# A new written order of the arithmetic: 39 crossbar entries in place of 24, and eleven stores on ScalarE's queue

## The chip, the core and the metric

The kernel runs on one core of a Trainium2 chip. The metric is the device time of one execution in microseconds; lower is better. The time before is the median of three runs.

The engines are named as the profile names them: PE is TensorE (PEld its weight loads), DVE is VectorE, ACT is ScalarE, POOL is GpSimd, SP is SyncE, which here does nothing but issue transfers. A name with a q (SPq, ACTq) is the part of an engine that issues transfers.

## The reference

Two layers follow each other. The first is a recurrence over 768 tokens, for 4 batches and 8 heads of width 40:

```python
for t in range(S):
    y[:, :, t] = np.einsum('bhd,bhde->bhe', rt, state)
    Sa = np.einsum('bhde,bhe->bhd', state, at)
    state_decay = state * wt[:, :, None, :] - np.einsum('bhd,bhe->bhde', Sa, bt)
    state = state_decay + np.einsum('bhd,bhe->bhde', vt, kt)
```

The second takes x, the heads side by side (4 x 768 x 320), and mixes tokens and channels:

```python
theta = x @ w_theta
zr, zi = x * np.cos(theta), x * np.sin(theta)
y = np.einsum('ts,bsd->btd', w_tok_r, zr) + np.einsum('ts,bsd->btd', w_tok_i, zi)
u = x + y
out = u + np.maximum(u @ w_ch, 0.0)
```

## The kernel before

Tokens are cut into chunks of 128, six for each batch, 24 in all, numbered 0 to 23. For each chunk the recurrence becomes matrix products: the inputs are scaled by running products of w (sums of logarithms, taken by matmul, then exponentials), transposed, multiplied to 128 x 128 score matrices (psi, phi, lamv, lamu), masked to a triangle, and used to form x0, nu, the new state gt and the output y. The state gt links a chunk to the next of its batch. The second layer follows for each chunk: theta, sine and cosine, z; when all six chunks of a batch have their z, the token mixing YR sums over them; then u, the channel product CH and the output.

What sets the order is one string, `ORDER`. An entry is a step, a chunk, an engine and a PSUM bank: `EVT:23S` is the step EVT of chunk 23 on SP; A is ACT, V is DVE, G is POOL, @n is a bank. The program walks the string once and emits each step's instructions; every engine then executes its own in that order and waits only for data and for free buffers. So the string sets what stands in front of what on each engine, and nothing else does.

A transpose can be made in two ways. On TensorE it is two entries: for v, `TRV` emits four 128 x 128 transposes into PSUM and `EVT` with A or V copies them out. With S there is no TRV; `EVT` is one crossbar transfer on SP (`dma_start_transpose`), from SBUF to SBUF. The same choice exists for nu (`NUT`, `ENUT`, four transposes), x (`XT`, `EXT`, three), u (`UT`, `EUT`, two for an even chunk and three for an odd one, which share the middle block), k and b (`TRK`, `EKBT`, eight), and the state (`GD`, `EGD`, four small matmuls). In the profile TensorE's transposes are those of line 316 (all other matmuls have line 312), and crossbar transfers stand at L488, L536 (v) and L701 (x and u).

`ST` stores a chunk's output `oo`, line 780, always on SP. Loads are `LDK`, `LDB`, `LDV`, `LDW`, `LDR` on SP and `LDA` mostly on ACT (lines 343 to 368). The order of all transfers is kept as written; an engine that comes to a transfer whose data are not ready waits there, with everything that stands behind it.

The helper that puts a transfer on an engine, and the choice of engine:

```python
def queue(e):
    return nc.scalar if e == "A" else nc.sync
```

Of the kernel before, what the change touches and what calls it, by code (L numbers as in the profile page):

```python
# [20 lines left out]
LDW:2 LN:2A LDW:0 CSI:2@1 LDK:0 INVW:2A CSE:2@0 LDA:1 LDC:0.0G LDC:0.2G CST:2 LN:0A WI:2A CSE:0@1  # L21
CST:0 LDA:0 CSI:0@0 WI:0A LDB:0 AH:1V LDB:1 LDK:1 LDK:2 AH:0V INVW:0A TRA:1@0 EAT:1V LDB:2 LDV:0
TRA:0@0 EAT:0A KH:0V TRK:0@3 KH:1V TRK:1@0 LDR:0 KH:2G LDA:2 EKBT:1A EKBT:0V PSI:0@0 PHI:0@1 EPSI:0V
LDV:1 LDB:3 CV:0A EPHI:0A LDK:3 LDA:3A MPHI:0G TRV:0@3 AH:2G X0:0@2 CR:0G LDV:2 ENX:0V PSI:1@0
PHI:1@1 LDW:4 NU:0 EVT:0V EPSI:1A ENU:0V LDR:2 TRK:2@0 EPHI:1V CV:1A EKBT:2A TRA:2@2 MPSI:1G EAT:2A
TRR:0@1 NUT:0@0 LDA:4A GT:0@2 ENUT:0V LDB:4 PSI:2@0 ERT:0A PHI:2@1 EGT:0V X0:1@0 LDK:4 GD:0@3 KH:3G
EPSI:2A EPHI:2V ENX:1A LDV:3 TRV:1@2 LDB:5 ERT:1A EGD:0A LV:0@0 CV:2A EVT:1V NU:1 ENU:1V LU:0@1
GT:1@1 GI:1 AH:3G ELU:0A LN:4A NUT:1@3 MPSI:2G TRV:2@2 LDA:5A MLU:0G LDK:5 TRA:3@0 ELV:0V ENUT:1V
LV:1@0 EAT:3V LU:1@1 LDR:4 EGT:1V TRK:3@3 GD:1@1 LDW:6 X0:2@0 ELV:1A ELU:1V EGD:1A EKBT:3V CR:2G
CSI:4@0 MLV:1G Y:0@1 ENX:2A INVW:4A NU:2 KH:4G EX:0V CSE:4@1 PSI:3@0 ENU:2A EVT:2A CST:4 WI:4A  # L30
TRR:2@1 LDA:6A GT:2@2 EPSI:3V NUT:2@3 ERT:2A ENUT:2V PHI:3@1 GI:2 ERT:3A AH:4G XT:0@3 CV:3G LU:2@0
EPHI:3V TRK:4@1 LV:2@1 AH:5G LDV:4 TRA:4@0 EXT:0A EGT:2V ELU:2A X0:3@2 TRV:3@3 LDK:6 EKBT:4A ELV:2V
ENX:3A LDB:6 Y:1@1 EAT:4A NU:3 PHI:4@0 ENU:3A EVT:3A MLU:2G PSI:4@1 EX:1V CR:4G NUT:3@2 EPHI:4V
KH:5G EPSI:4A LDV:5 LDK:7 ENUT:3A GT:3@1 MPSI:4G XT:1@0 Y:2@3 EGA:3V LV:3@0 EX:2V EGT:3V LU:3@1
EXT:1A TRR:4@0 TRA:5@1 ELV:3A LN:6A GD:3@2 TRK:5@3 ELU:3V EKBT:5A CSI:6@1 LDB:7 CV:4G ERT:4V EAT:5A
CSE:6@0 INVW:6A X0:4@3 GD:2@1 LDR:6 ENX:4A CST:6 ERT:5V WI:6A EGD:3V TRV:4@0 MLV:3G LDA:7A EGD:2V
EVT:4V KH:6G NU:4 AH:6G ENU:4A CV:5A PHI:5@1 PSI:5@0 EPSI:5A LDW:8 GT:4@2 EPHI:5V NUT:4@1 ENUT:4V
# [18 lines left out]
TRV:10@2 CR:10A EGT:9V TH:7@0 EPHI:10V EPSI:10V YR:0.4 ZR:5G ETH:7A TRR:10@1 LDK:12 EVT:10A LU:9@1
TRA:11@0 KH:11G CW:2.0G ERT:10A Y:8@2 EAT:11V YR:0.5 X0:10@0 LDB:12 ERT:11V LDV:11 LV:10@0 ELU:9A
EU:0V ENX:10A TRK:11@1 LN:12A NU:10 ELV:10V TH:6@3 CSE:12@1 CW:2.1G MLU:9G EX:8V ENU:10A EKBT:11V
CSI:12@0 CST:12 LDW:14 LDK:13 ETH:6A GT:10@2 WT:2.1@3 INVW:12A LDB:13 WI:12A WT:2.0@1 EWT:2.1V
EGA:10V LDA:13A Y:9@0 EWT:2.0A NUT:10@3 XT:8@1 PHI:11@1 KH:12G EGT:10V EXT:8A LDT:3.0 ENUT:10A  # L60
# [75 lines left out]
def kernel(  # L136
# [198 lines left out]
    def queue(e):  # L335
        return nc.scalar if e == "A" else nc.sync
# [569 lines left out]
```

## Time and profile before

| | us |
|---|---|
| median of 3 runs (202.24 to 202.73) | 202.59 |
| the profiled execution | 202.4 |
| its span | 200.7 |
| TensorE busy, share of the span | 186.6, 93% |
| VectorE busy | 168.7, 84% |
| ScalarE busy | 149.2, 74% |
| GpSimd busy | 146.5, 73% |

The busy time of TensorE contains overlap: matmuls are pipelined, so the pitch between two of them, and not the duration of one, says how much of the engine's queue each takes. A row of the timeline is: start, duration, engine, line, operation, written tile <- read tiles, shapes, count, and in brackets the idle time of the engine just before and what ended it. For an SPq or ACTq row the duration is that of issuing, not of the transfer. A row of a table of stretches is: from and to, length, then for each engine busy time and number of instructions, then granted TensorE clock, DMA share and GB/s. A row of waits is: who waited, for whom, microseconds in total, times, the longest. The granted clock was 1.00 throughout.

### The profile page before, as it was taken

To read this page: it belongs to the slowest core of one execution; us is meant where nothing else is said; L and a number is where in the kernel's file an instruction comes from. 1 tells how busy PE (TensorE), PEld (TensorE's weight loads), DVE (VectorE), ACT (ScalarE), POOL (GpSimd) and SP (SyncE) were. 2 spreads that over 40 slices of the span, in tenths; PEclk is the share of its full clock that TensorE was granted. 3 is DMA by queue.
4 is the path that set the end of the run, shared out by engine and by line. 5 is a ranking of instruction groups with operands and counts; after the bars stand their busy time and mean duration, and the time that the engine had idled before them with its cause. 6 is when DMAs were issued, how large, how long until landed. Compare 5 with 4: busy or idle time off the path is not lost.

```text
span 200.7 us, 7824 instructions
## 1 busy us (share of the span) xinstructions
PE 186.6 (93%) x3278; PEld 147.8 (74%) x3278; DVE 168.7 (84%) x319; ACT 149.2 (74%) x278; POOL 146.5 (73%) x155
## 2 busy tenths in 40 slices
PE   0769999999999999999999999999999999999992
PEld 0357788787888888888787878887877878776670
DVE  7257899899999998999899899899999876862682
ACT  4626999999999888898989686978688922682310
POOL 8118699789799998978998996963975986466000
PEclk9999999999999999999999999999999999999999
DMA  6999999999999999999987999994783596433434
GB/s 156 178 201 193 205 170 222 162 237 171 209 210 242 207 249 197 245 233 226 252 201 124 224 210 175 187 199 94 157 191 86 128 186 138 106 79 92 144 121 158
DMA packets 141955, 35.95 MB, mean 179 GB/s; under 512 B 136352, under 2 KB 140384, under 8 KB 141920
## 3 DMA queue, kind: packets, MB, share of 16 engines
q1 hardware_dynamic: 120064, 31.57, 76.8%
q10 hardware_dynamic: 20800, 3.28, 10.9%
q0 software_dynamic: 1056, 0.61, 2.3%
q8 instruction: 25, 0.41, 0.9%
q14 instruction: 10, 0.08, 0.1%
HBM read 29.54 MB, written 3.93 MB: 167 GB/s over the span
## 4 chain that ended last, share of the span: by engine, by line
PE 83%; SPq 5%; DVE 5%; DMA 4%; issue 1%; ACT 0%; DVEq 0%; ACTq 0%
PE sm L312 42%; PE sm L316 21%; PE sc L312 20%; DMA raw_kb<-in_k_dram 3%; SPq L363 1%; SPq L780 1%; DVE psi L309 1%; DMA xT<-x_two 1%; DVE phi L309 1%; SPq L368 1%; SPq L701 1%; DVE lamv L309 1%; DVE lamu L309 1%; SPq L357 1%; DVE kb L309 0%
## 5 line engine op out<-in xcount | busy, mean ns | idle before, releaser
L309 POOL TENSOR_TENSOR kb<-raw_kb,invW_two 128x640 bf16<-128x640 f32 x22 | 33.9, 1541 | 15.8 <-DMA raw_kb<-in_b_dram 8.2
L312 PE MATMUL sm<-z,wtok_r 128*128 128x320 bf16 x120 | 34.5, 300 | 0.0
L312 PE MATMUL sm<-z,wtok_i 128*128 128x320 bf16 x120 | 34.4, 299 | 0.0
L309 POOL TENSOR_TENSOR z<-cs,x_two 128x640 bf16<-128x640 f32 x22 | 30.8, 1402 | 2.2 <-ACT cs L739 1.9
L309 POOL TENSOR_TENSOR ah<-raw_a,Wi_two 128x320 bf16<-128x320 f32 x22 | 19.0, 864 | 8.5 <-issue 4.2
L309 DVE TENSOR_TENSOR psi<-sc,mask_p 128x1024 bf16<-128x1024 f32 x18 | 21.9, 1217 | 1.5 <-PE sc L312 1.5
L309 DVE TENSOR_TENSOR phi<-sc,mask_p 128x1024 bf16<-128x1024 f32 x16 | 19.5, 1219 | 1.6 <-PE sc L312 1.3
L309 DVE TENSOR_TENSOR lamu<-sc,mask_p 128x1024 bf16<-128x1024 f32 x15 | 18.3, 1219 | 0.5 <-PE sc L312 0.3
L312 PE MATMUL sc<-aT,kbT 64*128 64x128 bf16 x384 | 17.5, 225 | 0.0
L312 PEld LDWEIGHTS <-wtok_r 128*128 128x128 bf16 x144 | 14.0, 98 | 4.6
L312 PEld LDWEIGHTS <-wtok_i 128*128 128x128 bf16 x144 | 14.1, 98 | 3.4
L299 ACT COPY rvT<-sm 128x512 bf16<-128x512 bf16 (+1 forms) x26 | 12.7, 500 | 5.0 <-PE sm L316 4.9
L316 PE MATMUL sm<-ident,kb 128*128 128x128 bf16 x184 | 15.3, 231 | 1.1 <-DVE kb L309 1.1
L312 PE MATMUL sm<-kb,lamv 128*128 128x40 bf16 x192 | 15.0, 180 | 0.0
L312 PE MATMUL sm<-kb,lamu 128*128 128x40 bf16 x192 | 14.9, 179 | 0.0
L309 DVE TENSOR_TENSOR lamv<-sc,mask_p 128x1024 bf16<-128x1024 f32 x12 | 14.6, 1219 | 0.3
L312 PEld LDWEIGHTS <-rvT 64*128 64x128 bf16 (+1 forms) x272 | 13.5, 95 | 1.8 <-issue 0.3
L312 PEld LDWEIGHTS <-kbT 64*128 64x128 bf16 x384 | 11.8, 98 | 4.0 <-issue 2.3
L312 PE MATMUL sm<-wth,xT 128*128 128x320 bf16 x72 | 13.6, 300 | 0.8 <-DMA xT<-x_two 0.8
L776 DVE SCALAR_TENSOR_TENSOR oo<-sm,u_two 128x320 f32<-128x320 f32 x24 | 10.9, 489 | 3.6 <-PE sm L312 3.5
L309 DVE TENSOR_TENSOR x_two<-sm,Wi_two 128x320 bf16<-128x320 f32 x24 | 11.7, 486 | 2.5 <-PE sm L312 2.4
L594 POOL TENSOR_SCALAR_AFFINE_SELECT lamv<-lamv 128x1024 bf16<-128x1024 bf16 x12 | 13.1, 1092 | 0.9 <-ACT lamv L299 0.7
(137 smaller groups left out, 607.2 us busy)
## 6 DMA issues: line engine op xcount, KB each, us to landing
raw_w_two<-in_w_dram SPq DMA_DIRECT2D x12, 320.0 KB, 5.1
raw_kb<-in_k_dram SPq DMA_DIRECT2D x24, 160.0 KB, 5.0
raw_kb<-in_b_dram SPq DMA_DIRECT2D x24, 160.0 KB, 4.5
raw_v<-in_v_dram SPq DMA_DIRECT2D x24, 160.0 KB, 5.1
raw_r_two<-in_r_dram SPq DMA_DIRECT2D x12, 320.0 KB, 4.8
out_dram<-oo SPq DMA_DIRECT2D x24, 160.0 KB, 2.1
raw_a<-in_a_dram ACTq DMA_DIRECT2D x20, 160.0 KB, 4.7
wtok_raw<-in_moe_w_tok_r_dram SPq DMA_DIRECT2D x6, 384.0 KB, 4.9
```

Source lines behind the costliest of these rows:

```text
L299: keep(nc.scalar.copy(out=out, in_=in_))
L309: keep(eng[e].tensor_tensor(out=out, in0=in0, in1=in1, op=ALU.mult))
L312: keep(nc.tensor.matmul(out, lhsT=lhsT, rhs=rhs, start=start, stop=stop, skip_group_check=True))
L316: keep(nc.tensor.transpose(out=out, in_=in_, identity=ident))
L357: transfer(queue(e).dma_start(out=t, in_=two_of(w, i)))
L363: transfer(queue(e).dma_start(out=tiles[i].raw_kb[:, j], in_=source(ap, i)))
L368: transfer(queue(e).dma_start(out=t, in_=source(ap, i)))
L594: keep(nc.gpsimd.affine_select(out=flat, in_=flat, compare_op=ALU.is_ge, fill=0.0, base=-1, pattern=[[0, 2 * G], [1, 128]], channel_multip ...
L701: transfer(nc.sync.dma_start_transpose(out=t[:, 0:n], in_=held))
L776: keep(nc.vector.scalar_tensor_tensor(out=q.oo, in0=q.ops[:, 0:DM], scalar=0.0, in1=q.u, op0=ALU.max, op1=ALU.add))
L780: transfer(nc.sync.dma_start(out=out_r[i // NCH, i % NCH], in_=tiles[i].oo))
```

## The change

The string `ORDER` is replaced, so the arithmetic of all engines is written in another order, and `store` takes an engine. The order of the loads and the queues they are on are kept. Counted over the string:

- Crossbar entries (S): 39 in place of 24. v: chunks 18 to 23 (before 23 alone). nu: 18, 20, 21, 22 (before 20, 22). u: 2 and 4 to 18 (before 2, 10, 13 to 17 and 20). x: 13, 15 to 19, 21, 23 (before 15, 17 to 23). The states of 18, 20, 21, 22 and kb of 21 as before.
- TensorE has 48 transposes less: its queue has 6462 rows in place of 6558, a weight load and a matmul for each.
- Stores: eleven of 24 (chunks 1, 3, 4, 6, 7, 10, 12, 15, 16, 19, 23) on ACT, the rest on SP.
- Some evictions and products change their engine; two products ah go from DVE to POOL. The number of activation-table loads on ACT is 14 in both.

```diff
-LDW:2 LN:2A LDW:0 CSI:2@1 LDK:0 INVW:2A CSE:2@0 LDA:1 LDC:0.0G LDC:0.2G CST:2 LN:0A WI:2A CSE:0@1
...
+LDW:2 LN:2A LDW:0 CSE:2@1 LDK:0 LN:0A CST:2 CSE:0@0 CST:0 WI:2A CSI:2@1 LDA:1 LDC:0.0G LDC:0.2G
...
-    def store(i):
-        transfer(nc.sync.dma_start(out=out_r[i // NCH, i % NCH], in_=tiles[i].oo))
+    def store(i, e):
+        transfer(queue(e).dma_start(out=out_r[i // NCH, i % NCH], in_=tiles[i].oo))
...
-        "ST": lambda i, j, e, b: store(i),
+        "ST": lambda i, j, e, b: store(i, e),
```

Three places show what moves. First, VectorE at the beginning, from its first product on (kb_97 and ah_95 belong to chunk 0, kb_98 and ah_96 to chunk 1). Before:

```order
L309 TENSOR_TENSOR ah_96<-raw_a,Wi_two 128x8x40
L309 TENSOR_TENSOR ah_95<-raw_a,Wi_two 128x8x40
L301 COPY aT<-sm_276 128x512
L309 TENSOR_TENSOR kb_97<-raw_kb,invW_two 128x16x40
L309 TENSOR_TENSOR kb_98<-raw_kb,invW_two 128x16x40
L301 COPY kbT<-sm_294 128x1024
L309 TENSOR_TENSOR psi<-sc_322,mask_p 128x1024
```

Now:

```order
L308 TENSOR_TENSOR kb_97<-raw_kb,invW_two 128x16x40
L308 TENSOR_TENSOR kb_98<-raw_kb,invW_two 128x16x40
L308 TENSOR_TENSOR psi<-sc_311,mask_p 128x1024
L308 TENSOR_TENSOR phi<-sc_327,mask_p 128x1024
L308 TENSOR_TENSOR phi<-sc_382,mask_p 128x1024
```

The products ah have gone to GpSimd, and the copies of chunk 0's aT and kbT to ScalarE; between the two kb and the first psi VectorE has no copy any more.

Second, SyncE's queue in the stretch with the loads of chunks 20 and 21 (raw_kb_3765 in the old program and raw_kb_3757 in the new one are chunk 20's k and b, raw_kb_3839 and raw_kb_3943 chunk 21's). Before:

```order
L363 DMA raw_kb_3765<-in_k_dram 128x8x40
L368 DMA raw_v_3811<-in_v_dram 128x8x40
L701 DMA_TRANSPOSE xT_3826<-x_two_1_112 128x3x128
L363 DMA raw_kb_3765<-in_b_dram 128x8x40
L363 DMA raw_kb_3839<-in_b_dram 128x8x40
L780 DMA out_0_dram<-oo_3319 128x320
L363 DMA raw_kb_3839<-in_k_dram 128x8x40
L343 DMA raw_r_two_3980<-in_r_dram 128x8x80
```

Now:

```order
L362 DMA raw_kb_3757<-in_k_dram 128x8x40
L367 DMA raw_v_3771<-in_v_dram 128x8x40
L700 DMA_TRANSPOSE xT_3796<-x_two_1_112 128x3x128
L362 DMA raw_kb_3757<-in_b_dram 128x8x40
L700 DMA_TRANSPOSE uT_3854<-u_two_0_117 128x3x128
L700 DMA_TRANSPOSE uT_3861<-u_two_0_117 128x2x128
L487 DMA_TRANSPOSE nuT_3864<-nu_0_107 128x4x128
L535 DMA_TRANSPOSE rvT_3887<-v_3_106 128x4x128
L362 DMA raw_kb_3943<-in_b_dram 128x8x40
L362 DMA raw_kb_3943<-in_k_dram 128x8x40
L700 DMA_TRANSPOSE xT_3984<-x_two_2_113 128x3x128
L342 DMA raw_r_two_3986<-in_r_dram 128x8x80
```

Four more crossbar transfers now stand between chunk 20's b and chunk 21's, a fifth behind them, and the store between chunk 21's b and k is gone.

Third, SyncE's queue near the end, from chunk 14's and 15's u on (x_two_5_116 holds the x of chunks 22 and 23). Before:

```order
L701 DMA_TRANSPOSE uT_4952<-u_two_1_118 128x2x128
L701 DMA_TRANSPOSE uT_4957<-u_two_1_118 128x3x128
L701 DMA_TRANSPOSE xT_4999<-x_two_5_116 128x3x128
L780 DMA out_0_dram<-oo_4941 128x320
L780 DMA out_0_dram<-oo_4423 128x320
L701 DMA_TRANSPOSE xT_5077<-x_two_5_116 128x3x128
```

Now:

```order
L700 DMA_TRANSPOSE uT_4916<-u_two_1_118 128x2x128
L700 DMA_TRANSPOSE uT_4967<-u_two_1_118 128x3x128
L700 DMA_TRANSPOSE xT_4983<-x_two_5_116 128x3x128
L700 DMA_TRANSPOSE uT_5026<-u_two_2_119 128x2x128
L779 DMA out_0_dram<-oo_5018 128x320
```

Chunk 22's x is no longer on this queue (TensorE transposes it), and the two stores in front of chunk 23's x, those of chunks 12 and 8, are gone from there: 12's is on ScalarE, 8's stands earlier on SyncE.

More of the change, by code (lines that the diff above doesn't have):

```diff
@@ L26 @@
[L26 to L37, printed above, removed]
@@ L56 @@
[L56 to L60, printed above, removed]
-PSI:11@0 YR:2.0@1 EX:9V CV:11A EPSI:11V YR:2.1 XT:9@2 YR:2.2 TRV:11@0 EPHI:11A TRK:12@3 EXT:9V
@@ new lines @@
+LDK:21 PSI:19@0 CH:6@1 EXT:16S LDR:20 ZR:13G CHR:7@2 CH:7 Y:17@3 EPSI:19V LDA:21A LDW:22 KH:20G
+EPHI:19A MPHI:19G TRK:20@0 EO:6V EX:17V EKBT:20A KH:21G LDV:21 X0:19@1 CR:20G LU:18@0 LV:19@1
+EVT:20S ENX:19A YR:9.0@3 ELU:18A NU:19 YR:9.1 EGD:18S YR:9.2 CV:21G ENU:19A YR:9.3 ELV:19V YR:9.4
+EO:7V GT:19@1 LN:22A YR:9.5 TH:16@2 NUT:19@0 EKBT:21S EGA:19V EXT:17S MLU:18G PSI:20@0 ETH:16A
+PHI:20@1 EPSI:20A EU:9V EGT:19V YR:11.0@2 GD:19@3 LDK:22 EUT:8S ENUT:19V TRR:20@1 YR:11.1 Y:18@0
+EPHI:20V ERT:21V YR:11.2 ST:6A ZR:14G EX:18V LDA:22A MPSI:20G YR:11.3 LU:19@1 EGD:19V ELU:19V
@@ L132 @@
+CH:18@1 EU:21V CHR:19@2 CH:19 EO:18V EUT:20A YR:23.4 UT:21@3 YR:23.5 ST:17 EO:19V ST:16A UT:22@1
+CH:20@2 EU:23V EUT:21A EUT:22A CHR:21@3 ST:19A EO:20V CH:21 UT:23@0 CH:22@2 ST:18 ST:20 EUT:23A
+EO:21V ST:21 CHR:23@0 EO:22V CH:23 EO:23V ST:22 ST:23A
 """
```

192 lines of the change are left out of this document (100 added, 92 removed).

## The prediction

> **What bounds the kernel now.** I read the page's table of engines first, then stretches of ten microseconds (each engine's busy time, its instructions, the granted TensorE clock, the DMA share, GB/s), then the instructions in order of time at both ends.
>
> ```profile
> PE 186.6 (93%) x3278; PEld 147.8 (74%) x3278; DVE 168.7 (84%) x319; ACT 149.2 (74%) x278; POOL 146.5 (73%) x155
> ...
> 0.00:10.00 10.00, 3.88 (x38) 1.92 (x38) 5.22 (x45) 5.31 (x7) 4.97 (x16) 1.00 0.95 167
> 10.00:20.00 10.00, 8.06 (x97) 6.65 (x97) 6.37 (x10) 4.56 (x8) 5.17 (x5) 1.00 1.23 197
> ...
> 40.00:50.00 10.00, 9.70 (x196) 7.75 (x194) 9.77 (x17) 9.94 (x17) 9.27 (x10) 1.00 1.20 205
> ...
> 110.00:120.00 10.00, 10.00 (x192) 8.19 (x189) 9.01 (x17) 7.67 (x14) 9.22 (x9) 1.00 1.31 209
> ...
> 130.00:140.00 10.00, 10.00 (x184) 7.90 (x183) 9.46 (x15) 8.23 (x19) 4.96 (x7) 1.00 0.88 139
> ...
> 170.00:180.00 10.00, 10.00 (x162) 7.68 (x159) 7.83 (x12) 6.92 (x14) 4.99 (x4) 1.00 0.36 86
> 180.00:190.00 10.00, 9.20 (x83) 6.35 (x81) 3.85 (x8) 3.97 (x10) 3.89 (x3) 1.00 0.38 105
> 190.00:200.70 10.70, 6.91 (x58) 4.72 (x55) 6.66 (x16) 0.90 (x3) 0.00 (x0) 1.00 0.44 152
> ```
>
> The kernel has four parts. For 20 us TensorE is fed too slowly (8 us idle). From 20 to about 65 us it is nearly full, but so are VectorE, ScalarE and GpSimd (9.3 to 9.9 of 10 in the stretch shown), so there the matrix engine's pace is partly theirs. From 70 to 180 us it is full in every stretch at clock 1.00, with spare time on ScalarE: TensorE alone sets the end, and work taken off it there is worth its whole length if nothing new comes late. After 180 us gaps return; the last 3.6 us belong to the last output and its store.
>
> **What is taken off TensorE.** The order table has 15 more crossbar entries, and with them the groups of transposes for the same tiles go: v of chunks 18 to 22 (5 groups of 4), nu of 18 and 21 (2 of 4), u of 4 to 9, 11, 12 and 18 (22 blocks), less u of 20, which comes back (2). That is 20 + 8 + 22 - 2 = 48 transposes. Those of x change tiles, not number (13 and 16 go, 20 and 22 come). A transpose's price is its pitch, not its duration, since matmuls overlap:
>
> ```profile
> 97.45 0.61 PE L316 MATMUL sm<-ident,r 128*128 128x128 bf16 x8
> 97.89 0.30 PE L312 MATMUL sm<-z,wtok_r 128*128 128x320 bf16 x1
> ```
>
> Eight take 97.89 - 97.45 = 0.44 us of the queue, 0.055 each. So 48 x 0.055 = 2.6 us, nearly all of it between 105 and 175 us, where TensorE is full. **Term one: -2.6 us.** With them go 15 evictions (VectorE and ScalarE), which lie beside TensorE's work and which I count at nothing; if that cover were gone they would be worth more, not less.
>
> **What a crossbar transfer costs in its place.** It occupies SyncE's queue and then has to land.
>
> ```profile
> L701 SPq DMA_TRANSPOSE uT<-u_two x8: 1173/1186/1267, 106.6 to 192.0; - x8
> L701 SPq DMA_TRANSPOSE xT<-x_two x8: 1184/1202/2009, 126.8 to 184.4; - x8
> L780 SPq DMA_DIRECT2D out_dram<-oo x24: 332/510/2957, 115.7 to 197.7; - x24
> uT<-u_two SPq DMA_TRANSPOSE x8, 2.3
> xT<-x_two SPq DMA_TRANSPOSE x8, 4.0
> ```
>
> The first three rows are durations on the queue (least, median, most, in ns), the last two the median from issue to landing: 1.2 us of queue and 2.3 to 4.0 us to land. Added: 15 x 1.2 = 18 us of queue; taken away by eleven stores that move to ScalarE: 11 x 0.51 = 5.6 us. The dense place lies between the load of chunk 20's k and that of chunk 22's v, which before were issued here:
>
> ```profile
> 124.76 0.95 SPq L363 DMA_DIRECT2D raw_kb<-in_k_dram  x1
> ...
> 157.87 1.97 SPq L368 DMA_DIRECT2D raw_v<-in_v_dram  x1
> ```
>
> In these 33 us the queue had 7 crossbars, 12 loads and 6 stores; now it has 18, 12 and 3. At 1.2 us for a crossbar and about 0.55 for the rest that is 18 us before and 30 us now. It still fits, with 3 us to spare. Where it is tightest, chunk 21's k and b stand behind four or five crossbars in a row, that is up to 5 x 1.2 = 6 us later. Their user is GpSimd's kb, and behind that the crossbar of kb and TensorE's scores:
>
> ```profile
> 139.76 1.55 POOL L309 TENSOR_TENSOR kb<-raw_kb,invW_two 128x640 bf16<-128x640 f32 x1 [0.88 <-ACT invW_two L410]
> 142.84 1.24 SPq L488 DMA_TRANSPOSE kbT<-kb  x1
> 153.09 0.40 PE L312 MATMUL sc<-aT,kbT 64*128 64x128 bf16 x8
> ```
>
> From kbT's issue to its first score lie 10 us, so 6 us late at the load does not yet reach TensorE by this way. But not every crossbar is covered. Before, two of 24 were waited for, both at the end (next fence), with 0.58 and 0.53 us of stopped matmuls: 1.1 us over 24. At the same rate 15 more cost 15/24 x 1.1 = 0.7 us. Bounds: below, nothing; above, each of the 15 stops TensorE as long as the longer of the two, 15 x 0.58 = 8.7 us. I take 0.7, by the row nearest, since most of the new ones stand two or more microseconds of matmuls ahead of their users. **Term two: +0.7 us.**
>
> The Trainium skill speaks against the exchange: "VectorE: DVE Perf Modes", section "The three transpose paths", gives a 128x128 bf16 transpose 390 ns on TensorE and 1309 ns on the crossbar, and its rules prefer TensorE where the result may land in PSUM. The rows agree that a crossbar takes longer by itself. By those figures, estimated as time on the path, 48 blocks would add 48 x 0.919 = 44 us; the pitch and the slack above are why the sum does not go by it.
>
> **The stores on ScalarE.** Nearest row, a load issued there:
>
> ```profile
> 146.05 0.42 ACTq L368 DMA_DIRECT2D raw_a<-in_a_dram  x1
> ```
>
> 11 x 0.42 = 4.6 us of ScalarE's queue from 110 us on, where ScalarE has 1.8 to 3 us in ten to spare. Counted at nothing. What is queued behind a waiting store are ScalarE's evictions, on which TensorE depends; the stores stand 3 us of matmuls or more behind the output they read, except at the very end, so that wait should be over.
>
> **The end.** Here a transfer is now removed from in front of another.
>
> ```profile
> 184.24 0.30 PE L312 MATMUL sc<-z,wtok_i 128*128 128x320 bf16 x1
> 184.96 0.58 PE L312 MATMUL sm<-wth,xT 128*128 128x320 bf16 x3 [0.43 <-DMA xT<-x_two]
> ...
> 186.06 0.30 PE L312 MATMUL sm<-z,wtok_i 128*128 128x320 bf16 x1
> 186.73 0.45 PE L312 MATMUL sm<-wth,xT 128*128 128x320 bf16 x2 [0.37 <-DMA xT<-x_two]
> ...
> 195.75 0.43 PE L312 MATMUL sm<-wch,uT 128*128 128x320 bf16 x2
> 196.38 0.72 PE L312 MATMUL sm<-wch,uT 128*128 128x320 bf16 x4 [0.19 <-ACT uT L299]
> ...
> 182.12 0.49 DVE L309 TENSOR_TENSOR x_two<-sm,Wi_two 128x320 bf16<-128x320 f32 x1 [0.25 <-PE sm L312]
> 181.59 2.67 SPq L780 DMA_DIRECT2D out_dram<-oo  x2
> 184.36 1.18 SPq L701 DMA_TRANSPOSE xT<-x_two  x1
> ```
>
> Matmuls of 320 columns follow each other every 0.14 us, so these gaps cost 184.96 - 184.24 - 0.14 = 0.58 and 186.73 - 186.06 - 0.14 = 0.53 us. Chunk 23's x is ready at 182.61, but its crossbar issues at 184.36, 1.75 us late, behind two stores. In the new order those two stores stand elsewhere (one on ScalarE, one far earlier), and chunk 22's x goes through TensorE and VectorE instead of the crossbar. Both gaps can go, 1.1 us. A new gap remains possible: about 3 us of work now stand between chunk 23's x and its theta, against 2.3 to 4.0 us of landing. Bounds: 1.5 us gained (with the gap before 196.38, where two matmuls of 0.14 leave 0.35) and 0.8 lost. **Term three: -0.8 us.**
>
> **The beginning.** The arithmetic before the first score is rearranged.
>
> ```profile
> 11.84 1.03 PE L316 MATMUL sm<-ident,kb 128*128 128x128 bf16 x8 [0.72 <-DVE kb L309]
> 12.33 0.82 DVE L309 TENSOR_TENSOR kb<-raw_kb,invW_two 128x640 bf16<-128x640 f32 x1 [0.56 <-DMA raw_kb<-in_k_dram]
> 13.08 0.68 DVE L301 COPY kbT<-sm 128x1024 bf16<-128x1024 bf16 x1
> 13.22 1.03 PE L316 MATMUL sm<-ident,kb 128*128 128x128 bf16 x8 [0.35 <-DVE kb L309]
> 14.18 1.04 PE L312 MATMUL sc<-aT,kbT 64*128 64x128 bf16 x16
> 14.29 0.59 ACT L299 COPY kbT<-sm 128x512 f32<-128x512 f32 x1 [2.76 <-PE sm L316]
> 14.90 1.23 DVE L309 TENSOR_TENSOR psi<-sc,mask_p 128x1024 bf16<-128x1024 f32 x1 [1.14 <-PE sc L312]
> ```
>
> Chunk 0's kb waits for VectorE to finish chunk 1's kb before its copy, and its scores stand behind chunk 1's transposes. Now its copy is on the idle ScalarE and its scores come first: 11.84 + 1.03 + 0.59 = 13.5 us instead of 14.18 for the scores. That is 0.7 us on the first chunk's chain. Loads keep their order, and the other engines are nearly full soon after, so between nothing and all of it lasts; I take half. **Term four: -0.3 us.** Two more products move from VectorE to GpSimd; in the full stretch from 20 to 65 us that shifts load rather than removing it. Counted at nothing.
>
> **Sum.** The profiled execution took 202.4 us, 200.7 of them its span. -2.6 + 0.7 - 0.8 - 0.3 = -3.0, so 199.4; the median of the runs is 0.2 above that execution, so 199.6 us.
>
> **Rivals.** *First, crossbars that land late (slower, 205.0 us).* SyncE executes in order, so a crossbar whose source is late stops every load behind it; between 124 and 158 us it has 3 us to spare. It had such waits already:
>
> ```profile
> SPq L780 <- DVE oo L776: 5.2, 1, 5.2
> SPq L488 <- POOL r L301: 3.4, 1, 3.4
> ```
>
> The 5.2 us (a store) mostly go with the stores; waits like the 3.4 us (the crossbar of kb) become more frequent. The gains together are 3.7 us, so from 3.7 us of stops the change loses. If half of term two's upper bound comes true, 4.35 us, and a load is late by a wait like the 3.4 us of which half is covered, 1.7 us, the stops are 6.05 us in place of 0.7: 199.6 + 5.35 = 205.0. For it: the queue nearly full, and a DMA share of 1.31 at 110 us before anything is added. Against it: only 2 of 24 were felt so far. The mechanism is the slower transpose of the skill's rule above.
>
> *Second, nothing is won (202.5 us).* The transposes go, but SyncE's lag and ScalarE's store issues give back 3 us: the middle case between the sum and the first rival. For it: 30 of 33 us of queue; against it: ScalarE's spare time.
>
> *Third, the order gains all its bounds (197.8 us).* Terms one, three and four at their best, -2.6 - 1.5 - 0.7, and nothing late give 202.6 - 4.8 = 197.8. For it: each is a bound that a row shows; against it: all would have to come true together.
>
> **How the numbers follow.** My forecast 0.50, the third rival 0.18, the second 0.14, the first 0.18. The forecast's own range is 198.4 to 201.2. The whole range, leaving out a tenth at each side, is 197.0 to 204.2. A measurement of this kernel tells about 0.3% (0.6 us) from no change. Faster: the forecast, the third and a little of the second, 0.69. Same: most of the second, 0.11. Slower: 0.20.
>
> **What would show it.** TensorE with 3230 matmuls, its busy time about 3 us less, and full from 70 to about 176 us: term one. If the stretches from 110 to 170 us show TensorE below 9.9, with waits on rvT, nuT, uT or on raw loads, term two is too small. No gap before the last two thetas: term three. The first psi near 14.2 instead of 14.90: term four. ScalarE's stores waiting on oo, with evictions behind them, would make my zero for the stores wrong.

## The result: 210.63 us, and the profile after

The changed kernel takes 210.63 us (median of four executions, 210.47 to 213.21) against 202.42 us for the kernel before on the same chip. The ratio is 1.0435, with a 95% interval from 1.0388 to 1.0482: slower, outside the predicted range of 197.0 to 204.2. The profiled execution took 213.21 us, 211.5 of them its span; it is the longest of the four.

The page after, table of engines, and then the chain of waits by engine. (The chain before had PE 83%, SPq 5%, DVE 5%, DMA 4%.)

```profile
PE 187.6 (89%) x3230; PEld 145.2 (69%) x3230; DVE 163.4 (77%) x299; ACT 147.4 (70%) x278; POOL 147.6 (70%) x157
...
PE 53%; DMA 18%; SPq 12%; DVE 7%; issue 3%; ACT 3%; POOL 2%; POOLq 0%; ACTq 0%; DVEq 0%
```

The 48 matmuls are gone (3278 to 3230), yet TensorE fell from 83% of the chain to 53%; transfers and SyncE's queue took 30%. Where that happens is seen in the stretches:

```profile
40.00:50.00 10.00, 9.35 (x204) 7.59 (x204) 9.96 (x16) 9.53 (x20) 6.84 (x8) 1.00 1.05 193
...
130.00:140.00 10.00, 10.00 (x179) 7.86 (x176) 8.92 (x14) 8.56 (x16) 6.80 (x8) 1.00 1.30 170
140.00:150.00 10.00, 6.84 (x122) 5.15 (x121) 6.00 (x11) 3.19 (x5) 4.22 (x4) 1.00 0.84 152
150.00:160.00 10.00, 7.76 (x95) 5.43 (x90) 5.46 (x9) 6.41 (x10) 8.04 (x9) 0.66 1.02 183
170.00:180.00 10.00, 9.15 (x133) 6.98 (x135) 6.72 (x13) 4.48 (x9) 4.63 (x4) 1.00 0.80 171
180.00:190.00 10.00, 7.15 (x120) 5.01 (x120) 5.67 (x9) 4.79 (x10) 6.14 (x7) 1.00 0.57 89
```

Until 140 us little is wrong on TensorE. Between 140 and 160 TensorE stands still for 5.4 us and runs part of the rest at a lower granted clock (0.66); between 170 and 190 it loses another 3.7 us. Before, it was full from 130 to 180 at clock 1.00.

The waits, summed over the execution, name what came late (who waited, for whom, microseconds in total, times, the longest):

```profile
ACT lw_two L374 <- DMA raw_w_two<-in_w_dram: 10.9, 7, 5.1
POOL v L300 <- DMA raw_v<-in_v_dram: 9.7, 5, 3.1
POOL kb L308 <- DMA raw_kb<-in_k_dram: 9.7, 4, 5.1
```

These are 30 us of waits for loads, on ScalarE and GpSimd. A good part of them lies in the first 100 us and is no news: before the change, ScalarE's wait for `raw_w_two` was 2.0 us and GpSimd's for k 1.8, all of it there. From 100 us on the three rows hold 21.5 us, against 0.5 us before (one v). They aren't TensorE's waits, though. TensorE itself stops longest for results of crossbars:

```profile
142.30 0.99 PE L311 MATMUL sm<-wch,uT 128*128 128x320 bf16 x6 [1.46 <-DMA uT<-u_two]
149.09 0.58 PE L311 MATMUL sm<-wth,xT 128*128 128x320 bf16 x3 [1.70 <-DMA xT<-x_two]
189.23 0.40 PE L311 MATMUL sc<-rvT 64*128 64x128 bf16 x8 [2.08 <-DMA rvT<-v]
```

With one more of 0.49 us they come to 5.7 us. Another 3.5 us of TensorE's stops (2.23, 0.52 and 0.77) are behind loads that came late. Together that is nearly all of the 9.3 us that TensorE is idle between 140 and 190 us. The two kinds hang together: the rvT of the last row had to wait for the load of chunk 23's v, which was issued at 180.31 us. A stop behind a load, in order of time:

```profile
148.77 1.54 POOL L308 TENSOR_TENSOR kb<-raw_kb,invW_two 128x640 bf16<-128x640 f32 x1 [5.05 <-DMA raw_kb<-in_k_dram]
...
151.59 0.74 ACT L374 ACTIVATE lw_two<-raw_w_two 128x640 bf16<-128x640 f32 x1 [5.09 <-DMA raw_w_two<-in_w_dram]
152.23 0.41 ACT L298 COPY th<-sm 128x320 f32<-128x320 f32 x1
...
152.69 0.43 PE L311 MATMUL sm<-z,wtok_r 128*128 128x320 bf16 x1 [2.23 <-ACT th L298]
```

ScalarE executes in order, so for 5.09 us it stands at a logarithm whose w has not landed. Behind it stands the eviction of a theta, for which TensorE waits in turn. The load itself was issued late. SyncE's queue there, with the loads of chunk 21's k, of w and of chunk 22's k and v; first before, then after:

```profile
132.06 0.43 SPq L363 DMA_DIRECT2D raw_kb<-in_k_dram  x1
138.88 0.43 SPq L357 DMA_DIRECT2D raw_w_two<-in_w_dram  x1
145.44 0.57 SPq L363 DMA_DIRECT2D raw_kb<-in_k_dram  x1
165.88 0.58 SPq L368 DMA_DIRECT2D raw_v<-in_v_dram  x1
```

```profile
131.28 2.23 SPq L367 DMA_DIRECT2D raw_v<-in_v_dram  x1
...
135.97 0.58 SPq L362 DMA_DIRECT2D raw_kb<-in_b_dram  x1
136.66 4.17 SPq L700 DMA_TRANSPOSE uT<-u_two  x2
140.91 1.22 SPq L487 DMA_TRANSPOSE nuT<-nu  x1
142.23 1.21 SPq L535 DMA_TRANSPOSE rvT<-v  x1
143.49 0.57 SPq L362 DMA_DIRECT2D raw_kb<-in_b_dram  x1
144.12 0.57 SPq L362 DMA_DIRECT2D raw_kb<-in_k_dram  x1
144.79 1.47 SPq L700 DMA_TRANSPOSE xT<-x_two  x1
...
146.93 1.14 SPq L356 DMA_DIRECT2D raw_w_two<-in_w_dram  x1
...
154.81 0.57 SPq L362 DMA_DIRECT2D raw_kb<-in_k_dram  x1
...
170.79 0.69 SPq L367 DMA_DIRECT2D raw_v<-in_v_dram  x1
...
180.31 0.58 SPq L367 DMA_DIRECT2D raw_v<-in_v_dram  x1
```

Chunk 21's k goes out 12.1 us later than before, w 8.1, chunk 22's k 9.4, its v (157.87 before) 12.9, and chunk 23's v, the last load, 14.4. Of the 12.1 us, 5.9 were there when the stretch began: chunk 20's k goes out at 130.66 in place of 124.76, behind four of the added crossbars (two u, an x and a v between 122 and 131 us, 5.6 us of queue).

The queue is full. From chunk 20's k (130.66) to chunk 22's v (170.79) it needs 40.1 us for 33 transfers. Summed over its rows, the 18 crossbars take 28.0 us (1.55 each, not 1.2), the 14 loads and stores ahead of that v 9.9, and the pauses of about 0.07 us after each of these 32 make up the rest. That it is full by its own work, and doesn't stand waiting for late engines, is seen when each transfer's waits in the program are set against the trace's records of the semaphores. Between 120 and 190 us every transfer had all it waited for before its turn came: SyncE stood 0 us for a source, a tile or another transfer's landing. In the kernel before it stood 11.4 us there. So the rows longer than 1.2 us aren't waits for a source or a free tile either. The load of a v at 131.28 took 2.23 us, and its only wait had been over at 129.29. What makes them longer is not shown.

### The profile page after: what moved, and what is told of

The parts are those of the page before. It is cut to its first block, busy times and chain, and to the rows that moved or that the text cites. A ratio compares the mean times of both kernels' runs of the same rounds, so it can differ in the third digit from the quotient of the medians.

```text
span 211.5 us, 7752 instructions
## 1 busy us (share of the span) xinstructions
PE 187.6 (89%) x3230; PEld 145.2 (69%) x3230; DVE 163.4 (77%) x299; ACT 147.4 (70%) x278; POOL 147.6 (70%) x157
## 4 chain that ended last, share of the span: by engine, by line
PE 53%; DMA 18%; SPq 12%; DVE 7%; issue 3%; ACT 3%; POOL 2%; POOLq 0%; ACTq 0%; DVEq 0%
PE sm L311 28%; PE sc L311 13%; PE sm L315 11%; DMA raw_w_two<-in_w_dram 8%; SPq L362 4%; SPq L367 3%; DMA raw_kb<-in_b_dram 2%; DMA raw_a<-in_a_dram 2%; DMA rvT<-v 2%; DMA raw_v<-in_v_dram 2%; DMA uT<-u_two 2%; DVE psi L308 1%; DVE phi L308 1%; SPq L487 1%; ACT lamv L298 1%
## 5 line engine op out<-in xcount | busy, mean ns | idle before, releaser
L311 PE MATMUL sm<-z,wtok_r 128*128 128x320 bf16 x120 | 35.3, 306 | 2.2 <-ACT th L298 2.2
L308 POOL TENSOR_TENSOR z<-cs,x_two 128x640 bf16<-128x640 f32 x23 | 32.2, 1403 | 4.5 <-DVE xT L300 2.8
L308 POOL TENSOR_TENSOR ah<-raw_a,Wi_two 128x320 bf16<-128x320 f32 x24 | 20.8, 865 | 6.2 <-ACT Wi_two L451 2.5
L308 DVE TENSOR_TENSOR psi<-sc,mask_p 128x1024 bf16<-128x1024 f32 x17 | 20.7, 1219 | 3.5 <-PE sc L311 3.4
L308 DVE TENSOR_TENSOR phi<-sc,mask_p 128x1024 bf16<-128x1024 f32 x18 | 21.9, 1219 | 1.4 <-PE sc L311 1.0
L308 DVE TENSOR_TENSOR lamu<-sc,mask_p 128x1024 bf16<-128x1024 f32 x16 | 19.5, 1220 | 1.6 <-PE sc L311 1.4
L308 DVE TENSOR_TENSOR lamv<-sc,mask_p 128x1024 bf16<-128x1024 f32 x13 | 15.9, 1220 | 3.0 <-PE sc L311 2.8
L298 ACT COPY rvT<-sm 128x512 bf16<-128x512 bf16 (+1 forms) x32 | 15.7, 518 | 1.9 <-PE sm L315 1.1
L374 ACT ACTIVATE lw_two<-raw_w_two 128x640 bf16<-128x640 f32 x12 | 8.9, 739 | 11.0 <-DMA raw_w_two<-in_w_dram 10.9
L311 PEld LDWEIGHTS <-kbT 64*128 64x128 bf16 x384 | 11.9, 97 | 5.8 <-issue 2.2
L311 PE MATMUL sm<-wch,uT 128*128 128x320 bf16 x72 | 13.3, 300 | 2.1 <-DMA uT<-u_two 1.9
```

What stands on the lines that cost most here:

```text
L298: keep(nc.scalar.copy(out=out, in_=in_))
L308: keep(eng[e].tensor_tensor(out=out, in0=in0, in1=in1, op=ALU.mult))
L311: keep(nc.tensor.matmul(out, lhsT=lhsT, rhs=rhs, start=start, stop=stop, skip_group_check=True))
L374: keep(nc.scalar.activation(out=q.lw[:, :, :, 0:D], in_=q.raw_w.rearrange("p h (j d) -> p j h d", j=2), func=AF.Ln))
```

## The experiments

All ratios are to the kernel before, run on the same chip, with 95% intervals; 1% is 2.0 us. The theories are named in the expectations. Q and Q2: SyncE's queue holds up what stands behind the crossbars. D and R: the results of the crossbars themselves come late for TensorE. S: the stores hold up ScalarE. O: the new order itself costs the time.

**Stores.** The kernel before with the same eleven stores on ScalarE:

```diff
-ST:1
+ST:1A
```

> The kernel before with the same eleven stores on ScalarE's queue and nothing else. Theory Q: SyncE is freed a little, 201.5 to 202.8 us. Rival S: ScalarE waits for stores, 204 or more.

Measured 202.55 us, ratio 0.9999 (0.9966 to 1.0031). The zero for the stores was right. The reverse, the changed kernel with all stores on SyncE:

```diff
-ST:1A
+ST:1
```

> The changed kernel with all 24 stores back on SyncE's queue. Theory Q: SyncE has 11 x 0.5 = 5.5 us more to do, so loads are as late or later, 210 to 215 us. Rival S (stores on ScalarE hold up its evictions): ScalarE is freed, 203 to 207.

Measured 216.34 us, 1.0684 (1.0607 to 1.0761): 5.0 us worse than the change (2.5% of 202.4), by 11 stores that took 0.51 us each on the queue before, 5.6 us. More load on SyncE is worse; S falls.

**Loads moved ahead of the crossbars**, all still on SyncE:

```diff
-EUT:7S ERT:18A WI:20A ELU:17V EUT:6S ST:4A ENUT:18S Y:16@0 EVT:19S ... LDB:21
+LDB:21 LDK:21 LDR:20 LDW:22 LDV:21 EUT:7S ERT:18A WI:20A ELU:17V EUT:6S ...
```

> The changed kernel with one thing moved: on SyncE's queue the loads of chunks 20 to 23 stand ahead of the crossbar transfers they stood behind (b and k of 21, r of 20, w of 22 and v of 21 ahead of u of 7; k and b of 22 ahead of v of 20; r and v of 22 ahead of u of 8; the loads of 23 ahead of nu of 20). Crossbars, stores and arithmetic stay. Theory Q (loads come late because they queue behind crossbars, and ScalarE and GpSimd, which execute in order, sit in front of them): ScalarE's 5.1 us and GpSimd's 5.1 us of waiting for loads near 145 us go, the clock drop with them; 199 to 203 us. Rival D (39 crossbar transfers slow everything that is moved, or their results are late for TensorE): little changes, 208 to 211.

Measured 213.68 us, 1.0555 (1.0505 to 1.0606): worse than the change. As the expectation put it, this speaks against Q. The trace says what happened. The loads were early again (the last v at 165.4 us), and now crossbars were late:

```profile
164.05 0.57 SPq L362 DMA_DIRECT2D raw_kb<-in_k_dram  x1
164.67 0.73 SPq L367 DMA_DIRECT2D raw_a<-in_a_dram  x1
165.44 0.83 SPq L367 DMA_DIRECT2D raw_v<-in_v_dram  x1
166.38 1.47 SPq L487 DMA_TRANSPOSE nuT<-nu  x1
```

```profile
170.31 0.61 PE L311 MATMUL sc<-rvT,nuT 64*128 64x128 bf16 x8 [5.14 <-DMA nuT<-nu]
```

TensorE waits 5.14 us for one crossbar that stood behind the loads. So Q, which spoke of loads alone, became Q2: the queue as a whole is too full, and its order only decides who is late.

**Parts of the change, taken back or done alone.** Nine u back on TensorE in the changed order (transposes and copies put by hand into free places; this holds for the next two as well, and such places are not searched for):

```diff
-EUT:4S
+UT:4@1
...
+EUT:4A
```

> The changed kernel with u of chunks 4 to 9, 11, 12 and 18 transposed by TensorE again and copied by VectorE or ScalarE (30 crossbar entries in place of 39; 22 transposes more on TensorE, 1.2 us). Theory Q: SyncE's queue is 9 x 1.2 = 11 us shorter, most of it just ahead of the loads of 21 and 22; the stall near 145 us goes, the one near 185 us stays in part: 203 to 206 us. Rival D: 9 of 15 groups gone, so some 60% of the 8 us loss: 205.5. If the arithmetic's order itself is at fault: 210 or more.

Measured 207.62 us, 1.0275 (1.0210 to 1.0341).

v of 18 to 22 and nu of 18 and 21 back on TensorE, the u kept on the crossbar (32 crossbars):

```diff
-EVT:18S
+TRV:18@0
...
+EVT:18A
```

> The new order with v of 18 to 22 and nu of 18 and 21 back on TensorE, the nine u kept on the crossbar (32 in all). Theory Q2: 7 crossbars of 1.2 us and more leave the dense stretch from 125 to 185 us, some 10 us of its queue, so loads of chunks 21 and 22 come several us earlier: 204.0 to 207.5 us, at least as much won as by the nine u (3 us). Theory R: the results of v and nu are used soon after they are made and those of u late, so nearly all of the loss goes: 202.5 to 204.0 us. Theory O: 209 us or more.

Measured 205.41 us, 1.0107 (1.0039 to 1.0175). Seven of the 39 crossbars carry 3.3% of 4.35%. With all sixteen back:

> The new order with all 16 added crossbars (9 of u, 5 of v, 2 of nu) back on TensorE: 23 crossbars, stores still on ScalarE, the rest as changed. Theories Q2 and R: the loss goes, and what the order gains at both ends remains: 200.5 to 203.0 us. Theory O: the loss stays for the most part, 206 us or more. With 30 crossbars it was 207.6; one third of the loss gone for 9 crossbars would give 205 us if the loss were in proportion to their number.

Measured 208.71 us, 1.0250 (1.0192 to 1.0308). That is O's range, but O had 209 us or more for the run before this one. With 23 crossbars it is slower than with 32: in this order the nine u on the crossbar are a gain of 1.4% when v and nu are not there, and a loss of 1.6% when they are. A price for each crossbar by itself (R) can't say both; a queue that still has some room without the seven and none with them can. The traces bear that out: from 120 to 190 us SyncE stood 3.8 us with 32 crossbars and 21.6 us with 23, against nothing with 39. What the version with 23 loses is therefore not the queue: from 100 us on its TensorE waits for no crossbar, and loads are waited for by 0.7 us at most. Its TensorE is idle for 4.7 us between 20 and 140 us, where the kernel before has 1.4. How much of the 208.7 us belongs to places chosen by hand is not known.

The old order, with five v or nine u through the crossbar and nothing else:

```diff
-TRV:18@1 ... EVT:18A
+EVT:18S
```

> The old order with one part of the change alone: v of chunks 18 to 22 goes through the crossbar (5 more, 29 in all; 20 transposes less on TensorE, 1.1 us by the pitch). Theory Q2 (the crossbars fill SyncE's queue from about 125 us on, and whatever stands last in it is late): the stretch of 33 us in which the queue needed 18 us needs 24, it still fits: 201.0 to 203.5 us. Theory R (each crossbar result reaches TensorE late by itself, whatever the queue's load): five results at 0.5 us or more each, 204.0 us or more. Theory O (the new order of the arithmetic costs the time, not the crossbars): 201.5 us.

Measured 206.68 us, 1.0178 (1.0106 to 1.0250): R's range, more than Q2 had.

```diff
-UT:4@1 ... EUT:4V
+EUT:4S
```

> The old order with nine u (chunks 4 to 9, 11, 12, 18) through the crossbar: 33 in all, 22 transposes less on TensorE (1.2 us). Theory Q2: where they stand in the old order (from about 108 to 160 us) they add 11 us to a queue that had 15 us of slack in 33, a near fit: 202 to 206 us. Theory R: the results are needed at the next CH step, a few us later in this order: 205 us or more. Theory O: 201.5 us.

Measured 211.78 us, 1.0404 (1.0334 to 1.0474), R's range again. In the old order TensorE does wait for these results directly (a row of the view of waits):

```profile
PE sm L311 <- DMA uT<-u_two: 4.7, 4, 2.0
```

The loads are late in both runs too (the last v goes out 5.8 us later than before with the five v, 10.3 us with the nine u). But here the queue isn't full: SyncE stood 9.3 and 9.5 us between 120 and 190 us.

**Crossbars that nobody waits for** separate the queue from the results. A ghost sends the same tile at the same place through the crossbar into a tile that nothing reads:

```diff
+    def ghost(i, held):
+        t = ghosts.pop(0)
+        ghosts.append(t)
+        n = held.shape[1] // 128
+        transfer(nc.sync.dma_start_transpose(
+            out=t.rearrange("p (a b) -> p a b", b=128)[:, 0:n], in_=held))
...
+DVT:18
```

First the version with 32 crossbars (205.41 us), with seven ghosts in place of the seven that were taken out:

> The order of the run with v and nu on TensorE (205.4 us), and seven crossbars that nobody waits for: v of 18 to 22 and nu of 18 and 21 are also sent through the crossbar, at the places where the changed order has them, into tiles that nothing reads. SyncE's queue is that of the changed kernel, TensorE waits for none of the seven. Theory Q2 (the queue: what stands behind the crossbars comes late): most of the 5.2 us between 205.4 and the changed kernel's 210.6 come back, 208.5 to 211 us. Theory R (the seven results themselves come late for TensorE): 204.5 to 206.5 us.

Measured 213.46 us, 1.0533 (1.0476 to 1.0589), above even Q2's range: 4.3% more, 8.6 us, with no result that anybody could wait for. R can't explain it. The queue tells how it works. The same five loads, without ghosts and with them:

```profile
127.95 0.58 SPq L362 DMA_DIRECT2D raw_kb<-in_k_dram  x1
...
136.91 0.69 SPq L362 DMA_DIRECT2D raw_kb<-in_k_dram  x1
...
148.78 0.57 SPq L362 DMA_DIRECT2D raw_kb<-in_k_dram  x1
...
163.39 0.70 SPq L367 DMA_DIRECT2D raw_v<-in_v_dram  x1
...
170.64 0.58 SPq L367 DMA_DIRECT2D raw_v<-in_v_dram  x1
```

```profile
128.53 1.21 SPq L826 DMA_TRANSPOSE wtok_raw<-v  x1
129.78 0.58 SPq L363 DMA_DIRECT2D raw_kb<-in_k_dram  x1
...
141.86 0.57 SPq L363 DMA_DIRECT2D raw_kb<-in_k_dram  x1
...
153.58 0.58 SPq L363 DMA_DIRECT2D raw_kb<-in_k_dram  x1
...
169.71 0.70 SPq L368 DMA_DIRECT2D raw_v<-in_v_dram  x1
...
178.04 0.58 SPq L368 DMA_DIRECT2D raw_v<-in_v_dram  x1
```

They are 1.8, 5.0, 4.8, 6.3 and 7.4 us later, with 1, 3, 4, 5 and 6 ghosts in front of them. At the 1.2 us of a crossbar that would be 1.2, 3.6, 4.8, 6.0 and 7.2, which is near. With the ghosts SyncE again stands for nothing from 120 to 190 us, and without them it stood only 1.0 us between the first and the last of these loads. So there was next to no slack to absorb them: about a crossbar's time on the queue passes to all loads behind it, and that of seven (8.4 us) to the end. The 8.6 us are known to 1.8 either way. Some of them may be TensorE's clock: in three of the four executions the granted clock was 0.984 to 0.992. The one at 1.00 took 211.73 us, 7.7 us above the execution at 1.00 of the version without ghosts, or 1.10 for each.

The same seven as plain copies:

```diff
-        transfer(nc.sync.dma_start_transpose(
-            out=t.rearrange("p (a b) -> p a b", b=128)[:, 0:n], in_=held))
+        transfer(nc.sync.dma_start(out=t[:, 0:128 * n], in_=held))
```

> As the run with seven ghost crossbars (213.46 us against 205.41 without them), but the seven are plain copies of the same tiles to the same places, which hold SyncE's queue for about 0.57 us each, as a load or a store does, in place of 1.23. Theory Q3 (with 32 crossbars the queue of SyncE is full from 110 to 190 us, so each further transfer moves all loads behind it by its own time on the queue, and the end by the same): 205.4 + 7 x 0.6 = 209.6 us, between 208.5 and 210.8. Theory W (it is not the time on the queue: each ghost makes the queue wait for its source to be written, which a copy does as a crossbar does): 212.5 us or more. Theory X (a crossbar at work slows or blocks other transfers, a copy does not): 205.5 to 207.5 us.

Measured 208.61 us, 1.0260 (1.0197 to 1.0324): 1.5% above the version without ghosts, 3.1 us, 0.44 (0.27 either way) for each copy against 1.23 (0.26) for each crossbar. That is near Q3's number and the copies' time on the queue; W (the wait for sources) falls, also because SyncE stood for nothing with the seven crossbars. Q3's premise, a queue already full with 32, is nearly so up to the last load (1.0 us of standing) and less so behind it (2.9 us). And the trace, of the slowest of the four executions (210.79 us), doesn't show the step between: there the same five loads go out 2.5 to 7.1 us later than without ghosts, about as with crossbars, though six copies took only 4.4 us of queue. So what a transfer costs beyond its own row is open. The interval reaches down to 206.4 us, so X is not quite excluded.

In the old order, nine ghosts for the nine u:

```diff
 EUT:4V
+DUT:4
```

> The kernel before with nine crossbars that nobody waits for: u of chunks 4 to 9, 11, 12 and 18 goes into tiles that nothing reads, right behind the copy from TensorE's transposes, which stay. The same nine used in earnest gave 211.8 us. Theory Q2: 207 us or more, since loads and the other crossbars are behind them just the same. Theory R: 202.3 to 204 us, since nobody waits for the nine.

Measured 207.09 us, 1.0220 (1.0164 to 1.0276): Q2's edge, and about half of the 4.0% that the nine cost in earnest. By size, then, the queue and the late results share the loss in the old order. There the ghosts left SyncE 3.7 us of standing between 120 and 190 us, where it had 11.4 without them.

**Room made in the queue.** The 16 loads of k, b, v, w and r of chunks 20 to 23 on ScalarE's queue, first in the changed kernel:

```diff
-LDK:20
+LDK:20A
```

> The changed kernel with the 16 loads of k, b, v, w, r of chunks 20 to 23 on ScalarE's queue in place of SyncE's, at their places in the order. They no longer stand behind crossbars, and SyncE's queue has some 9 us less. ScalarE has 16 x 0.42 = 6.7 us more to issue. Theory Q2: raw loads are no longer late and the crossbars come earlier: 203 to 207 us. Theory R: the results of the crossbars are late by their own landing of 2.5 to 4.5 us: 209 us or more.

Measured 207.88 us, 1.0276 (1.0207 to 1.0345): 1.6% won, within neither range quite as stated, nearer Q2's. The same in the version with 32 crossbars:

> The new order with 32 crossbars (v of 18 to 22 and nu of 18 and 21 on TensorE: 205.4 us) and the 16 loads of k, b, v, w, r of chunks 20 to 23 on ScalarE's queue. Theory Q3: at 32 crossbars the queue is still full and sets the loads' times, so taking 16 x 0.6 us of loads off it gains: 200.5 to 203.5 us. Theory O (what is left over the kernel before is the order of the arithmetic, not the queue): 205 us or more.

Measured 208.96 us, 1.0311 (1.0252 to 1.0370), O's range, and 2% worse than without the move, which O doesn't explain either. In both runs SyncE stands 6 or 7 times, up to 5.8 us in all between 100 and 200 us, for the landing of another transfer; without the move it never does. And in the old order with five v crossbars:

> The kernel before with the two new ends (201.6 us), v of 18 to 22 through the crossbar (28 in all; alone in the old order this cost 3 us) and the 16 loads of chunks 20 to 23 on ScalarE's queue. Theory Q3: the 5 crossbars then cost nothing on the queue, and 20 transposes x 0.055 = 1.1 us less on TensorE come through: 200.3 to 201.6 us. Theory R (v's results come late by their landing): 203.5 us or more.

Measured 211.84 us, 1.0460 (1.0418 to 1.0502): far off. ScalarE's queue is not free of SyncE's. Each transfer gets one of eight completion semaphores in turn, in written order over both queues, and the program lets it wait for the landing of the last transfer that had the same one. Two rows of this run's program:

```
L357 DMA raw_w_two_3703<-in_w_dram 128x8x80 [waits DMAHW3_49]
...
L780 DMA out_0_dram<-oo_3318 128x320 [waits DMAHW3_49]
```

The first is on ScalarE, the second is the next on SyncE that has this semaphore:

```profile
129.18 0.38 ACTq L357 DMA_DIRECT2D raw_w_two<-in_w_dram  x1
```

```profile
129.37 2.24 SPq L701 DMA_TRANSPOSE xT<-x_two  x1
134.22 0.36 SPq L780 DMA_DIRECT2D out_dram<-oo  x1
```

The load's record of landing is at 134.20; SyncE stands from 131.61 to 134.22 before a store, 2.6 us, and a crossbar of v stands behind it. So a load that ScalarE issues late (it comes to it in its own order) stops SyncE too. This is one place; that all 10 us of this run come from it is not shown.

Stores were moved next, since nobody waits for them. All of the changed kernel's stores on ScalarE:

```diff
-ST:0
+ST:0A
```

> The changed kernel with its other 13 stores on ScalarE's queue too (39 crossbars kept). The opposite of the run with all stores on SyncE, where 11 more stores cost 5.7 us, 0.52 each. Theory Q3 (SyncE's queue is full, so what is taken off it comes off the end): some eight of the 13 stand before the last loads and crossbars, so 8 x 0.55 = 4.4 us less than 210.6: 204.5 to 208 us. Theory C (what counts is the eight completion semaphores that all transfers share in written order, so that moving a transfer to another queue helps nothing): 210 us or more.

Measured 210.06 us, 1.0342 (1.0283 to 1.0401): 0.6 us less than the change by the medians, 1.9 by the ratios. By its number this is C. But the eight stores of the expectation were a miscount: only three of the 13 stand between chunk 20's k and chunk 22's v, 1.7 us of queue, so the run doesn't tell C from Q3. With 32 crossbars:

> The new order with 32 crossbars (205.4 us), all 24 stores on ScalarE's queue. Theory Q3: if the queue is what is left of the loss, 202.0 to 204.5 us; if the queue with 32 is no longer the bound, as before, 205 to 206 us. Theory C: 205 us or more.

Measured 205.97 us, 1.0157 (1.0117 to 1.0197): nothing won, C's range or Q3's second, though SyncE now stood 9.5 us between 120 and 190 us. So what the version with 32 crossbars still loses is not shown to be the queue. Part of it lies earlier: between 20 and 140 us its TensorE is idle 2.8 us, 1.4 more than before the change.

**The two ends**, in the kernel before:

```diff
-EXT:22S
+XT:22@0
...
+EXT:22V
...
-ST:12
+ST:12A
```

> The kernel before with the change's two ends alone: the first 70 entries in the new order, chunk 22's x through TensorE in place of the crossbar, the store of chunk 12 on ScalarE and that of 8 earlier (16, 19 and 23 on ScalarE too), all else as before: 23 crossbars. By terms three and four of the prediction 202.6 - 0.8 - 0.3, so 201.0 to 201.9 us. If both ends give nothing: 202.4 us. Theories Q2 and R say the same here.

Measured 201.59 us over twelve executions, 0.9957 (0.9930 to 0.9983). This is the one version that beats both kernels: 0.9 us less than before. With five v crossbars and all stores off SyncE on top of it:

> The kernel before with the two new ends (201.6 us), v of 18 to 22 through the crossbar and all 24 stores on ScalarE's queue: SyncE has 5 crossbars more (6.1 us) and 20 stores less (10 us) than there. Theory Q3: SyncE is no busier than before the change, so the 20 transposes x 0.055 = 1.1 us come through: 200.3 to 201.8 us. Theory R (v's results come late by their landing, whatever the queue): 203 us or more, as when the five were added alone (206.0 by its ratio).

Measured 202.74 us, 1.0011 (0.9988 to 1.0034), between the ranges. With room in the queue the five v cost 0.5% in place of 1.8%, and the loads are as early as before (last v at 165.1 us). But the 1.1 us of transposes do not come through: against the version with the ends alone, 1.1 us are lost. Small waits of TensorE for results of ScalarE (0.57, 0.43 and 0.24 us at 176.5, 196.0 and 154.6) are part of it; the rest is open.

## Why the prediction was wrong, by its own steps

- **Term one** (-2.6): the 48 transposes are gone as said. Their worth could be read only where the matrix engine stays full, which after 140 us it doesn't; where the queue has room, with five v, it didn't show in the time, and small waits of TensorE (1.2 us) are part of why.
- **The step that failed** is in the part on the crossbar's cost, "18 us before and 30 us now. It still fits, with 3 us to spare", and with it **term two** (+0.7, at most 8.7). Between the same two loads the queue needed 40.1 us. Each crossbar was priced at the median of its duration, 1.2 us; in the full queue it took 1.55 on average (6.4 us in all), and a load or store 0.71 in place of 0.55 (2.2 us). The pauses between transfers (2.2 us) were left out. Why the rows are longer there is open; waits for a source or a tile it is not. The stretch was also priced as if the queue came to it on time, and it came 5.9 us late.
- The second half of the step, chunk 21's loads "up to 5 x 1.2 = 6 us later", which "does not yet reach TensorE": its k was 12.1 us later. The five crossbars themselves were priced about right (6.2 us were added within the stretch); the 5.9 us from ahead of it were left out. GpSimd's kb and ScalarE's logarithm waited 5 us each, and TensorE behind them.
- **The upper bound of term two**, 8.7 us, priced TensorE's own waits for crossbar results. Those were 5.7 us in the trace, inside the bound but far above the 0.7 that was taken. What the bound left out are the stops behind late loads (3.5 us) and the half clock from 151.2 us on (some 2.7 us, an estimate from the busy time at half clock, see the last section): 11.9 us together. With the ends worth -0.9, the loss of 8.8 us by the ratio asks for about 10 us of stops, and up to 12 if term one came through in full.
- **The first rival** named the outcome, loads held up behind crossbars in SyncE's order, and gave it 0.18. The cause that it gave, a crossbar whose source is late, did not occur in the dense stretch: SyncE stood there for no source at all, and it was the crossbars' own time on the queue that held up the loads. Its price, 1.7 us for one load half covered, was too small: seven crossbars alone are 8 us. It was priced as if the queue still had slack.
- **Term three** (-0.8) and **term four** (-0.3): together the old order gained 0.9 us from them (0.3 to 1.4), 1.1 expected. In the changed kernel the last two thetas wait for nothing, and the first psi starts at 13.99 in place of 14.90; but by TensorE's idle time the lead at 20 us (7.7 us idle, before 8.1) is gone at 40 us (9.1, before 9.0). From 20 to 140 us, where no term was set for the new order, TensorE is idle for 3.1 us, before 1.4.
- **Stores on ScalarE at nothing**: right (0.9999), though ScalarE's spare time from 110 us on was 1.0 to 6.7 us in ten, and not the 1.8 to 3 that were read.
- **Of the prediction's own signs**, TensorE below 9.9 with waits on uT and raw loads came true from 140 us on (6.84 and 7.76). Its busy time did not fall by 3 us (187.6, before 186.6), as 5.3 us of it ran at half the clock.
- **The skill's rule** (the Trainium skill, "VectorE: DVE Perf Modes", section "The three transpose paths", whose table has TensorE's path as the quicker one, 390 against 1309 ns) gave the right direction. The size that the prediction estimated from it, 44 us as time on the path, was far off: the run where seven crossbars hit a full queue gives 1.2 us for each, about their time on the queue.

What stays open: the 2.2 us (0.8 to 3.5) that the new order with 32 crossbars loses to the kernel before. Taking stores off the queue did not touch it; TensorE's 1.4 us more of idle time between 20 and 140 us is part of it, and the places of the transposes put back by hand may be. What makes the queue's rows longer in the dense stretch is open too. A third tile for xT and uT had no room in SBUF and wasn't tried; in the changed kernel it couldn't help from 120 to 190 us, where no crossbar waited for a tile to come free.

## What to carry to other kernels

Before work is moved to a queue that executes in order, add up that queue's whole need, from where the additions begin to the end of the densest stretch, from rows of that stretch and with the pauses, and leave slack: here 30 us were reckoned for 33, and 40.1 were needed. Then look in the trace for how long the queue stands waiting. A queue that never waits is full, and a transfer added to it costs everything behind it about its own time or more. A ghost, the same transfer into a tile that nothing reads, measures that cost apart from the lateness of the result. In these runs, moving the urgent loads in front, or to a second queue that shares completion semaphores with the first, mostly changed who is late.

## What the runs showed of the hardware that was not expected

The granted clock fell to a half in the middle of several runs, for 3.4 or 6.8 us, always just after TensorE had been idle. After, at 151.2 us (columns as in the tables of stretches):

```profile
147.80:151.20 3.40, 1.36 (x23) 1.06 (x24) 1.84 (x4) 0.00 (x0) 2.26 (x2) 1.00 1.20 219
151.20:154.60 3.40, 1.91 (x16) 1.57 (x16) 0.58 (x2) 3.00 (x4) 1.61 (x3) 0.50 1.35 223
154.60:158.00 3.40, 3.40 (x34) 2.00 (x33) 2.30 (x4) 1.55 (x4) 3.40 (x3) 0.50 0.90 145
```

The run with the loads on ScalarE, and the old order with five v, where it did not fall:

```profile
149.00:152.40 3.40, 1.60 (x29) 1.01 (x28) 1.75 (x4) 2.42 (x5) 2.63 (x3) 1.00 1.04 215
152.40:155.80 3.40, 3.40 (x29) 2.13 (x29) 2.12 (x4) 2.15 (x4) 3.40 (x4) 0.50 0.49 126
```

```profile
187.90:191.30 3.40, 1.73 (x14) 1.02 (x13) 0.49 (x1) 0.00 (x0) 0.83 (x1) 1.00 0.35 114
```

I cut each profile into windows of 3.41 us from its first rise of the clock on and summed TensorE's idle time in each, over all 20 profiles. All nine windows in the middle of a run that were followed by half the clock had 1.80 us idle or more (up to 3.02); the most idle one that was not, at full clock, had 1.67. So in these runs about half a window of idleness was enough. The Trainium skill ("TensorE: Matmul & The Clock Gate", section "Part 1: The HAM clock gate") has a free-running window of 3413 ns and a half clock after at least one idle window; the lengths of 3.4 and 6.8 us agree with it, but the windows here were still 12 to 47% busy. In the profiled execution after, TensorE was busy 5.3 us at half the clock, which makes the stops some 2.7 us longer (an estimate: half of these 5.3 us). Stops that are spread out need not bring it: with the seven ghosts TensorE lost 6.4 us between 140 and 190 us in gaps of up to 2.0 us, and the clock stayed at 1.00.
